# A planner's cost numbers, and with them the order of all instructions, in a linear-attention + MLP kernel on one core

## The chip, the core and the metric

One core of a Trainium2 chip runs the whole program. The metric is the device time of one execution in microseconds (us). Engines: PE (TensorE: matmul, and PEld, its weight loads), DVE (VectorE), ACT (ScalarE), POOL (GpSimd) and SP (SyncE, which issues the transfers). Each engine works through its own queue in order, and waits on semaphores for what others have to finish.

## The reference

```python
def _attn_ref(q, k, v, omega):              # q, k, v: 8 x 8 heads x 576 x 64, omega: 128 x 64
    q_s, k_s = q * scale, k * scale         # scale = 64 ** -0.25
    def phi(x):
        proj = np.einsum('bhsd,md->bhsm', x, omega)
        h = proj - np.sum(x * x, axis=-1, keepdims=True) / 2.0
        h = h - np.max(h, axis=-1, keepdims=True)
        return np.exp(h) / np.sqrt(m)
    q_p, k_p = phi(q_s), phi(k_s)
    kv = np.einsum('bhsm,bhsd->bhmd', k_p, v)
    z = np.sum(k_p, axis=2)
    num = np.einsum('bhsm,bhmd->bhsd', q_p, kv)
    den = np.einsum('bhsm,bhm->bhs', q_p, z)[..., None] + 1e-06
    return num / den

def _moe_ref(x, w_in, w_out):               # x: 4608 x 512 (the attention's output), d_ff 2048
    h = x @ w_in
    g = np.where(h > 0.0, h, np.exp(np.minimum(h, 0.0)) - 1.0)
    return g @ w_out
```

## The kernel before

The 64 heads are worked in 32 pairs. Two batches of four pairs each give a block row of tokens, whose attention output, transposed, is the input x of the MLP. The stages overlap, and by the clock of the profile they are roughly these.

- **Start, 0 to 40 us.** Pairs 0 to 7 are "native": q and k arrive as fp32 on 64 partitions (`load_pair`, L448). For each of a pair's two heads the square of x is written beside it (L483 on ACT, or through the helper of L394 on DVE or POOL), PE projects both with omega (L504, tiles `ppk` and `ppq`, one PSUM bank for each group of four 128-row pieces), DVE takes the row minimum of the negated scores (L512, `nbk`, `nbq`), ACT takes the exponentials (L474, `hk`, `hq`), PE forms K'V (L673, L678, `pkv`) and the sums z (L721, `pz`), DVE the denominators (L740), and PE the numerators (L794, `pn`).
- **Weights, 5 to 160 us.** The MLP weights arrive as 64-bit words and are turned into fp32 (L904 to L935), and split into a rounded high part and a low part.
- **MLP blocks, 120 to 770 us.** Eight blocks of 384 tokens. For each of 16 slices of d_ff: 12 matmuls of 384 columns into `ph` (L983 to L985, high and low parts), the ELU (L992 and L993 on ACT, L996 on DVE), `g` and its low part (L1001, L1004), and 9 matmuls of 512 columns into `acc` (L1017 to L1019).
- **Pairs 8 to 31, beside the MLP blocks.** Here q and k are split into high and low parts too (`tk`, `tq`): the high part is a cast, and the low part, "y_lo", is x minus the high part, 64x576, through the helper of L394, 96 in all (two heads, q and k, 24 pairs). PE projects at L554, DVE takes the row minimum with a product at L568, POOL adds biases (L579, L580), PE forms K'V at L622, z at L718 and the numerators at L842.
- **Last super-blocks, 770 to 1007 us.** The other 1536 tokens go in three blocks of 512 by a Strassen-like scheme, eight steps (j) each. A step computes products into PSUM tiles `A` and `B` (L1369, six matmuls of 256 columns a group; L1339 adds the second layer's part), combines them (`c`, L389 and L1393; L1324 clears the tiles), takes the ELU (L1417, L1422, L1425), splits the seven results `gq` into a high part (cast, ACT) and a low part (helper of L394, POOL or DVE), and multiplies each with its weights into seven sums `acs_1` to `acs_7` (L1527). Their input weights are prepared mostly on DVE from 680 us on (`rw`, `tw`, L394).

**What sets the order.** No instruction order is written out by hand. Every operation is a task that `op()` of the class `Plan` records: an engine and its cost in ns, a due time in us, the tiles it reads and writes, and for some tasks a second engine with its own cost and a handicap (`alt`, table `ALT`). `Plan.order()` walks a simulated clock: on each engine that is free it takes, of the tasks whose inputs are ready, the one with the earliest due time; `mine()` gives a task with two engines to the one that would end it earlier, handicap counted. DVE tasks marked `port` and POOL tasks are not started over each other. Transfers go one after the other through a single channel, with a latency `DMA_LAT` in front, a rate `DMA_RATE` in bytes per ns and a latency behind. Then `issue()` emits all tasks in the order of their simulated starts, and the engines' queues on the chip keep that order whatever the real durations are. So a cost changes nothing in the work: it changes what stands before what on each queue, and, for tasks with an `alt`, the engine.

Of the kernel before, what the change touches and what calls it, by code (L numbers as in the profile page):

```python
# [18 lines left out]
P = 128  # L19
B, H, S, D, M = 8, 8, 576, 64, 128  # L20
# [48 lines left out]
LAG = 3.4  # L69

# [61 lines left out]
class Plan:  # L132
# [14 lines left out]
    DMA_LAT, DMA_RATE = 1100.0, 360.0  # L147
# [33 lines left out]
    def order(self):  # L181
# [7 lines left out]
        end = [0.0] * len(tasks)  # L189
# [3 lines left out]
        slots, dma = {}, 0.0  # L193
# [41 lines left out]
        while len(done) < len(tasks):  # L235
            started = False
            for eng, q in queue.items():
# [37 lines left out]
                if nbytes:  # L275
                    dma = max(now + self.DMA_LAT, dma) + nbytes / self.DMA_RATE
                    end[best] = dma + self.DMA_LAT
                else:
                    end[best] = now + ns
# [34 lines left out]
def mm(n, m=1):  # L314

    return m * (n / 2.4 + 2.5)
# [10 lines left out]
def pool(n):  # L327
    return 40 + 2.33 * n
# [3 lines left out]
def performer_elu_kernel(  # L332
# [52 lines left out]
    op = pl.op  # L385
# [57 lines left out]
    def load_pair(i, due):  # L443
# [7 lines left out]
        for nm, nat, mixed in (("k", k, kx), ("q", q, qx)):  # L451
            if native(i, nm):
                t = s["x" + nm] = Buf(sb, [P, 2, S], F32, "ld" if nm == "k" else "t", f"x{nm}_{i}", 2)
                dma(lambda t=t: t()[0:D], nat[i], P * S * 4, (t, 0), (t, 1))
            else:
                t = s["x" + nm] = Buf(sb, [P, 2, S], F32, "ld", f"x{nm}_{i}", 2)
                dma(lambda t=t: t(), mixed[i - NNAT[nm]], P * S * 8, (t, 0), (t, 3))
# [6 lines left out]
    def project(i, nm, due):  # L464
# [14 lines left out]
        if native(i, nm):  # L479
# [11 lines left out]
            for g in range(3):  # L491
# [17 lines left out]
                op("PE", 872 if g < 2 else 240, d, mms, [*((x, a, 2) for a in range(2)), of], (p,))  # L509
# [21 lines left out]
        for a in range(2):  # L531
# [8 lines left out]
                "POOL", pool(S), due - 4 + a,  # L540
# [3 lines left out]
        for c in range(5):  # L544
# [14 lines left out]
            op("PE", mm(256, n), d, mms, [(y, a, z) for a in range(2) for z in "hl"] + ["oh", "om"], (p,))  # L559
# [14 lines left out]
            if c in (1, 4):  # L574
# [7 lines left out]
                op("POOL", 2 * pool(4), d + 1.3, bias, [sq, *((nb, g, e) for e in range(5))], ((nb, g),))  # L582
# [28 lines left out]
    def kv_swapped(i, due):  # L611
# [15 lines left out]
        op("PE", 5 * 216, due, mms, [*parts, v], (p,))  # L627
# [19 lines left out]
        op("POOL", 3 * pool(2 * M) + 2 * pool(M), due + 0.5, sums, parts, (zs, (zu, 1)))  # L647
# [13 lines left out]
    def kv(i, due):  # L661
# [22 lines left out]
        op("PE", 220, due, last, [*parts, v], ((p, 0), (p, 1)))  # L684
# [17 lines left out]
    def finish(i, due):  # L702
# [25 lines left out]
        for g in range(3):  # L728
# [48 lines left out]
            op("PE", 109 * n, d, turn, ((h, "n", g),), (p,))  # L777
# [19 lines left out]
        op("PE", 4 * mm(S) + 200, d, mms, [*((qh, g) for g in range(3)), ("kvf", i % 2)], [p for _, _, p in halves])  # L797
# [29 lines left out]
    def output(i, qt, due):  # L827
# [8 lines left out]
        def mms():  # L836
# [10 lines left out]
            "PE", 4 * mm(4 * N) + 200, due, mms, [*((qt, g) for g in range(3)), *((zk, "kv", e) for e in range(4))], banks  # L847
# [869 lines left out]
```

## Time and profile before

| what | value |
|---|---|
| time, median of 3 runs (lowest, highest) | 1003.58 us (1001.74, 1006.97) |
| the profiled execution, its own time | 1008.6 us |
| its span in the profile | 1006.8 us |
| PE granted clock, mean | 0.996 of full speed |
| HBM traffic over the span | 223 GB/s |

The profiled execution is one run, 5.0 us above the median; what is read from it is a place or a difference, and the sum has to be brought to the median at the end. A share of busy time is read by stage, as the stages have different limits: for each stage, the length less PE's busy time is what any order could at most win there.

### The profile page before, as it was taken

To read this page: it belongs to the slowest core of one execution; us is meant where nothing else is said; L and a number is where in the kernel's file an instruction comes from. 1 tells how busy PE (TensorE), PEld (TensorE's weight loads), DVE (VectorE), ACT (ScalarE), POOL (GpSimd) and SP (SyncE) were. 2 spreads that over 40 slices of the span, in tenths; PEclk is the share of its full clock that TensorE was granted. 3 is DMA by queue.
4 is the path that set the end of the run, shared out by engine and by line. 5 is a ranking of instruction groups with operands and counts; after the bars stand their busy time and mean duration, and the time that the engine had idled before them with its cause. 6 is when DMAs were issued, how large, how long until landed. Compare 5 with 4: busy or idle time off the path is not lost.

```text
span 1006.8 us, 24315 instructions
## 1 busy us (share of the span) xinstructions
PE 979.3 (97%) x7806; PEld 881.6 (88%) x7806; DVE 843.7 (84%) x3077; ACT 766.2 (76%) x2064; POOL 557.8 (55%) x745
## 2 busy tenths in 40 slices
PE   6999999999999999999999999999999999999997
PEld 5887889888888888888888888887888999999997
DVE  5999978786778967887889888889999889779766
ACT  5999876877568888788887878786555688877774
POOL 0667676776457676677667766685442232223221
PEclk8999999999999999999999999999999999999999
DMA  6656777857766777676776767666888885775762
GB/s 178 181 183 214 238 247 254 270 200 245 232 216 218 232 224 225 202 230 195 252 226 189 242 206 234 203 208 232 268 311 290 289 298 176 238 240 191 239 196 76
DMA packets 93264, 226.27 MB, mean 225 GB/s; under 512 B 23056, under 2 KB 35024, under 8 KB 93136
## 3 DMA queue, kind: packets, MB, share of 16 engines
q1 hardware_dynamic: 93136, 224.70, 69.0%
q8 instruction: 63, 1.03, 0.4%
q14 instruction: 65, 0.53, 0.2%
HBM read 187.43 MB, written 37.22 MB: 223 GB/s over the span
## 4 chain that ended last, share of the span: by engine, by line
PE 69%; DVE 16%; DMA 8%; ACT 3%; issue 2%; SPq 1%; POOL 1%; DVEq 0%; POOLq 0%; ACTq 0%
PE acs L1527 8%; PE ph L983 7%; PE ph L985 6%; PE ph L984 6%; PE acc L1017 6%; PE acc L1018 6%; PE acc L1019 6%; PE A L1369 5%; PE B L1369 4%; PE pn L842 3%; PE pkv L622 2%; PE ppq L554 2%; PE ppk L554 2%; DVE rw L394 2%; DMA rw<-w1s 1%
## 5 line engine op out<-in xcount | busy, mean ns | idle before, releaser
L983 PE MATMUL ph<-xh,w1c 128*128 128x384 f32 x512 | 176.8, 345 | 4.6 <-DVE g L1004 3.0
L984 PE MATMUL ph<-xl,w1c 128*128 128x384 f32 x512 | 172.3, 336 | 1.0 <-DVE xl L807 1.0
L985 PE MATMUL ph<-xh,w1c 128*128 128x384 f32 x512 | 172.3, 336 | 0.0
L1017 PE MATMUL acc<-w2h,g 128*128 128x512 f32 x384 | 154.3, 402 | 0.2
L1018 PE MATMUL acc<-w2l,g 128*128 128x512 f32 x384 | 151.6, 395 | 0.0
L1019 PE MATMUL acc<-w2h,g 128*128 128x512 f32 x384 | 151.5, 394 | 0.0
L983 PEld LDWEIGHTS ph<-xh,w1c 128*128 128x128 f32 x512 | 96.2, 188 | 17.0 <-DVE g L1004 7.3
L984 PEld LDWEIGHTS ph<-xl,w1c 128*128 128x128 f32 x512 | 96.3, 188 | 3.8 <-DVE xl L807 1.4
L992 ACT ACTIVATE e<-ph 128x384 f32<-128x384 f32 x128 | 62.6, 489 | 44.4 <-PE ph L985 43.4
L394 POOL TENSOR_TENSOR hq<-hq,den 128x512 f32<-128x512 f32 (+1 forms) x96 | 81.1, 854 | 27.3 <-DVE den L749 23.5
L985 PEld LDWEIGHTS ph<-xh,w1c 128*128 128x128 f32 x512 | 96.2, 188 | 0.0
L996 DVE SCALAR_TENSOR_TENSOR ph<-e,ph 128x384 f32<-128x384 f32 x128 | 71.2, 556 | 25.5 <-ACT e L993 24.3
L394 POOL TENSOR_TENSOR gq<-yh,gq 128x256 fp32r<-128x256 f32 x49 | 42.7, 871 | 85.1 <-ACT gq L389 67.0
L1019 PEld LDWEIGHTS acc<-w2h,g 128*128 128x128 f32 x384 | 72.1, 188 | 16.9
L1017 PEld LDWEIGHTS acc<-w2h,g 128*128 128x128 f32 x384 | 72.0, 188 | 16.3 <-issue 6.3
L740 DVE CUSTOM_DVE_ANT_0 junk<-hq,pz 128x128 f32<-128x128 f32 (+1 forms) x320 | 74.5, 279 | 11.6 <-PE pz L718 9.3
L394 POOL TENSOR_TENSOR tk<-xk,tk 64x576 fp32r<-64x576 f32 x45 | 64.1, 1424 | 31.5 <-ACT tk L389 12.6
L474 ACT ACTIVATE hk<-hk,nbk 128x128 f32<-128x128 f32 x216 | 68.4, 390 | 17.0 <-POOL nbk L580 16.7
L1018 PEld LDWEIGHTS acc<-w2l,g 128*128 128x128 f32 x384 | 72.1, 188 | 8.6
L474 ACT ACTIVATE hq<-hq,nbq 128x128 f32<-128x128 f32 x216 | 68.5, 391 | 14.4 <-POOL nbq L580 13.6
L394 POOL TENSOR_TENSOR tq<-xq,tq 64x576 fp32r<-64x576 f32 x46 | 65.8, 1431 | 23.6 <-ACT tq L389 11.5
L1004 DVE TENSOR_TENSOR g<-ph,g 128x384 fp32r<-128x384 f32 x128 | 70.4, 550 | 5.7 <-PE pn L842 1.8
(222 smaller groups left out, 2814.7 us busy)
## 6 DMA issues: line engine op xcount, KB each, us to landing
w1c<-w1s SPq DMA_DIRECT2D x112, 512.0 KB, 4.5
wp<-w1t SPq DMA_DIRECT2D x48, 512.0 KB, 4.0
raw_w<-in_w_dram SPq DMA_DIRECT2D x32, 512.0 KB, 4.3
xk<-in_kx_dram SPq DMA_DIRECT2D x24, 576.0 KB, 4.2
xq<-in_qx_dram SPq DMA_DIRECT2D x24, 576.0 KB, 4.7
wp<-w1s SPq DMA_DIRECT2D x24, 512.0 KB, 4.5
v<-in_v_dram SPq DMA_DIRECT2D x32, 325.0 KB, 3.3
w1s<-w1c SPq DMA_DIRECT2D x16, 512.0 KB, 4.2
```

The costliest lines, as they stand in the source:

```text
L394: (nc.vector if e == "DVE" else nc.gpsimd).tensor_tensor(*args)
L474: nc.scalar.activation(h()[:, j, :], src(j), AF.Exp, bias=nb()[:, j:j + 1], scale=-1.0)
L740: nc.vector.tensor_tensor_reduce(out=junk()[r], in0=h()[r, j, :], in1=pz()[r, a * P:(a + 1) * P], scale=1.0, scalar=EPS, op0=ALU.mult, op1 ...
L983: nc.tensor.matmul(ph(), wh, xh[:, c, o:o + n], start=(c == 0), stop=False)
L984: nc.tensor.matmul(ph(), wh, xl[:, c, o:o + n], start=False, stop=False)
L985: nc.tensor.matmul(ph(), wl, xh[:, c, o:o + n], start=False, stop=(c == NC - 1))
L996: lambda: nc.vector.scalar_tensor_tensor(ph(), e()[:, 0:n], -1.0, ph(), ALU.add, ALU.max), (p, e), (p,),
L1017: nc.tensor.matmul(a(), g[0]()[:, ts], w2h[:, f], start=(f == f0), stop=False)
L1018: nc.tensor.matmul(a(), g[0]()[:, ts], w2l[:, f], start=False, stop=False)
L1019: nc.tensor.matmul(a(), g[1]()[:, ts], w2h[:, f], start=False, stop=(f == f1 - 1))
L1369: nc.tensor.matmul(o, at(a, i), u[b][:, i], start=(start and fresh_bank and i == 0 and n == 0), stop=(i == 1 and n == 2), skip_group_check ...
L1527: nc.tensor.matmul(bank()[:, z * TH:(z + 1) * TH], g()[:, a * TH + z * P:a * TH + z * P + P], w(b), start=(j == 0 and z == 0 and m == 0), ...
```

## The change

Only numbers that the planner uses are changed, and one constant is new. A transfer now takes 500 ns in front, 320 bytes per ns, and 2450 ns (`DMA_POST`) behind it, where it had 1100 ns, 360 bytes per ns and 1100 ns; loads of native q and k are planned with twice their bytes. `mm()` gives 113.4 ns for a matmul of 256 columns (109.2 before), 173.1 for 384 (162.5) and 232.9 for 512 (215.8); the tasks of PE that had a number of their own get larger ones. `pool()` and POOL's own numbers change: y_lo is now 1495 ns on POOL (`pool(576)` was 1382). Costs on DVE and ACT stay as they were (y_lo on DVE: 669 ns, and a handicap of 820).

```diff
+DMA_POST = 2450.0
...
-    DMA_LAT, DMA_RATE = 1100.0, 360.0
+    DMA_LAT, DMA_RATE = 500.0, 320.0
...
                     dma = max(now + self.DMA_LAT, dma) + nbytes / self.DMA_RATE
-                    end[best] = dma + self.DMA_LAT
+                    end[best] = dma + DMA_POST
...
 def mm(n, m=1):
-    return m * (n / 2.4 + 2.5)
+    return m * (0.467 * n - 6.2)
...
 def pool(n):
-    return 40 + 2.33 * n
+    return 120 + 2.22 * n
...
-                dma(lambda t=t: t()[0:D], nat[i], P * S * 4, (t, 0), (t, 1))
+                dma(lambda t=t: t()[0:D], nat[i], P * S * 8, (t, 0), (t, 1))
...
-                op("PE", 872 if g < 2 else 240, d, mms, [*((x, a, 2) for a in range(2)), of], (p,))
+                op("PE", 930 if g < 2 else 290, d, mms, [*((x, a, 2) for a in range(2)), of], (p,))
...
-                "POOL", pool(S), due - 4 + a,
+                "POOL", 1495, due - 4 + a,
                 lambda e, r=r, o=o, cs=cs: tt(e, y()[o, cs], x()[r, 0], y()[r, cs].bitcast(F32), ALU.subtract),
                 (*parts, (y, a, "h")), ((y, a, "l"),), alt=other("y_lo", "DVE", dve(S)), port=True,
...
-            op("PE", mm(256, n), d, mms, [(y, a, z) for a in range(2) for z in "hl"] + ["oh", "om"], (p,))
+            op("PE", 118 * n + 10, d, mms, [(y, a, z) for a in range(2) for z in "hl"] + ["oh", "om"], (p,))
...
-                op("POOL", 2 * pool(4), d + 1.3, bias, [sq, *((nb, g, e) for e in range(5))], ((nb, g),))
+                op("POOL", 550, d + 1.3, bias, [sq, *((nb, g, e) for e in range(5))], ((nb, g),))
...
-        op("PE", 5 * 216, due, mms, [*parts, v], (p,))
+        op("PE", 1340, due, mms, [*parts, v], (p,))
...
-        op("POOL", 3 * pool(2 * M) + 2 * pool(M), due + 0.5, sums, parts, (zs, (zu, 1)))
+        op("POOL", 3480, due + 0.5, sums, parts, (zs, (zu, 1)))
...
-        op("PE", 220, due, last, [*parts, v], ((p, 0), (p, 1)))
+        op("PE", 240, due, last, [*parts, v], ((p, 0), (p, 1)))
...
-            op("PE", 109 * n, d, turn, ((h, "n", g),), (p,))
+            op("PE", 115 * n + 20, d, turn, ((h, "n", g),), (p,))
...
-        op("PE", 4 * mm(S) + 200, d, mms, [*((qh, g) for g in range(3)), ("kvf", i % 2)], [p for _, _, p in halves])
+        op("PE", 1250, d, mms, [*((qh, g) for g in range(3)), ("kvf", i % 2)], [p for _, _, p in halves])
...
-            "PE", 4 * mm(4 * N) + 200, due, mms, [*((qt, g) for g in range(3)), *((zk, "kv", e) for e in range(4))], banks
+            "PE", 1400, due, mms, [*((qt, g) for g in range(3)), *((zk, "kv", e) for e in range(4))], banks
```

The added line at the top and one blank line move every later line by two: L474 of before is L476 of the changed kernel, L394 is L396, and so on. Three places in the order follow. A name carries the pair (`xk_1` is K of pair 1), the group (`ppk_1_0` is group 0 of pair 1) and a running number.

**First place: ACT at the start.** Before, the square of pair 1's K stands ahead of the exponentials of pair 0:

```order
L483 ACTIVATE xk_0_162<-xk_0_162 64x576
L398 ACTIVATE of_133<-of_133 64x128
L483 ACTIVATE xq_0_173<-xq_0_173 64x576
L483 ACTIVATE xk_1_177<-xk_1_177 64x576
L474 ACTIVATE hk_0_216<-ppk_0_0_191,nbk_0_205 128x128 x4
L474 ACTIVATE hk_0_216<-ppk_0_1_200,nbk_0_205 128x128 x4
L474 ACTIVATE hk_0_216<-ppk_0_2_211,nbk_0_205 128x128
```

Now the exponentials come first, and ACT no longer squares pair 1's K at all (DVE does both heads):

```order
L485 ACTIVATE xk_0_162<-xk_0_162 64x576
L400 ACTIVATE of_133<-of_133 64x128
L485 ACTIVATE xq_0_173<-xq_0_173 64x576
L476 ACTIVATE hk_0_213<-ppk_0_0_195,nbk_0_207 128x128 x4
L476 ACTIVATE hk_0_213<-ppk_0_1_202,nbk_0_207 128x128 x4
L476 ACTIVATE hk_0_213<-ppk_0_2_209,nbk_0_207 128x128
L485 ACTIVATE xq_1_179<-xq_1_179 64x576
```

**The same place on PE.** Before, the projection of pair 1 (`ppk_1_0`, `ppk_1_1`) stands ahead of K'V of pair 0:

```order
L504 MATMUL ppk_0_0_191<-of_133,xk_0_162 128x128 x4
L504 MATMUL ppk_0_1_200<-of_133,xk_0_162 128x128 x4
L504 MATMUL ppk_0_2_211<-of_133,xk_0_162 64x128 x2
L504 MATMUL ppk_1_0_228<-of_133,xk_1_177 128x128 x4
L504 MATMUL ppk_1_1_235<-of_133,xk_1_177 128x128 x4
L673 MATMUL pkv_0_246<-v_0_175,hk_0_216 128x130
L678 MATMUL pkv_0_246<-v_0_175,hk_0_216 128x65 x8
```

Now half of K'V of pair 0 stands ahead of `ppk_1_0`, and the other half behind it:

```order
L506 MATMUL ppk_0_0_195<-of_133,xk_0_162 128x128 x4
L506 MATMUL ppk_0_1_202<-of_133,xk_0_162 128x128 x4
L506 MATMUL ppk_0_2_209<-of_133,xk_0_162 64x128 x2
L675 MATMUL pkv_0_228<-v_0_175,hk_0_213 128x130
L680 MATMUL pkv_0_228<-v_0_175,hk_0_213 128x65 x4
L506 MATMUL ppk_1_0_236<-of_133,xk_1_177 128x128 x4
L680 MATMUL pkv_0_228<-v_0_175,hk_0_213 128x65 x4
L506 MATMUL ppk_1_1_249<-of_133,xk_1_177 128x128 x4
```

**Second place: the low part y_lo in pairs 8 to 31.** Before, POOL computes both heads of pair 21's K (`x2`):

```order
L394 TENSOR_TENSOR hq_18_6070<-hq_18_6070,den_18_6408 128x128
L394 TENSOR_TENSOR tq_20_6507<-xq_20_6284,tq_20_6507 64x576
L579 TENSOR_TENSOR nbk_20_6576<-nbk_20_6576,sqk_20_6333 128x4
L580 TENSOR_TENSOR nbk_20_6576<-nbk_20_6576,sqk_20_6333 128x4
L394 TENSOR_TENSOR tk_21_6611<-xk_21_6448,tk_21_6611 64x576 x2
L579 TENSOR_TENSOR nbk_20_6576<-nbk_20_6576,sqk_20_6333 128x5
L580 TENSOR_TENSOR nbk_20_6576<-nbk_20_6576,sqk_20_6333 128x5
```

Now POOL has one of the two:

```order
L582 TENSOR_TENSOR nbq_19_6392<-nbq_19_6392,sqq_19_6017 128x5
L396 TENSOR_TENSOR tq_20_6514<-xq_20_6227,tq_20_6514 64x576 x2
L581 TENSOR_TENSOR nbk_20_6560<-nbk_20_6560,sqk_20_6194 128x4
L582 TENSOR_TENSOR nbk_20_6560<-nbk_20_6560,sqk_20_6194 128x4
L396 TENSOR_TENSOR tk_21_6628<-xk_21_6484,tk_21_6628 64x576
L581 TENSOR_TENSOR nbk_20_6560<-nbk_20_6560,sqk_20_6194 128x5
```

and the other stands on DVE, between the row minima of pair 20 and the ELU of slice 70:

```order
L570 ISA nbk_20_6560 128x1
L570 ISA hk_20_6559,nbk_20_6560<-ppk_20_4_6602,p2k_20_4_6621 128x128
L570 ISA nbk_20_6560 128x1
L396 TENSOR_TENSOR tk_21_6628<-xk_21_6484,tk_21_6628 64x576
L998 SCALAR_TENSOR_TENSOR ph_70_6605<-e_70_6643,ph_70_6605 128x384
L393 COPY qt_18_6500<-pn_18_1_6648 128x4x32
L393 COPY qt_18_6500<-pn_18_1_6648 64x32
```

Over all, DVE has 5 of the 96 such instructions before and 31 now.

**Third place: PE, where the super-blocks begin.** Before, the first sum, `acs_1` (of `gq_0_0_1`: super-block 0, step 0, part 1), stands behind the last six matmuls of layer 2 and two groups of step 1 (`wp_0_1_0`):

```order
L1019 MATMUL acc_7_0_0_10798<-w2h_140,g_127_1_11574 128x512
L1369 MATMUL B_11586<-xh_147,wp_0_0_2_11535 128x256 x6
L1369 MATMUL A_11549<-xh_147,wp_0_1_0_11601 128x256 x6
L1017 MATMUL acc_7_0_1_10808<-w2h_140,g_127_0_11566 128x512
L1018 MATMUL acc_7_0_1_10808<-w2l_141,g_127_0_11566 128x512
L1019 MATMUL acc_7_0_1_10808<-w2h_140,g_127_1_11574 128x512
L1017 MATMUL acc_7_0_2_10817<-w2h_140,g_127_0_11566 128x512
L1018 MATMUL acc_7_0_2_10817<-w2l_141,g_127_0_11566 128x512
L1019 MATMUL acc_7_0_2_10817<-w2h_140,g_127_1_11574 128x512
L1369 MATMUL B_11586<-xh_147,wp_0_1_0_11601 128x256 x6
L1527 MATMUL acs_1_11714<-w2h_140,gq_0_0_1_11676 128x256
```

Now it stands ahead of all of them:

```order
L1529 MATMUL acs_1_11671<-w2l_141,gq_0_0_1_11634 128x256
L1529 MATMUL acs_1_11671<-w2h_140,gq_0_0_1_11634 128x256 x2
L1529 MATMUL acs_1_11671<-w2l_141,gq_0_0_1_11634 128x256
L1529 MATMUL acs_1_11671<-w2h_140,gq_0_0_1_11634 128x256
L1019 MATMUL acc_7_0_1_10813<-w2h_140,g_127_0_11574 128x512
L1020 MATMUL acc_7_0_1_10813<-w2l_141,g_127_0_11574 128x512
L1021 MATMUL acc_7_0_1_10813<-w2h_140,g_127_1_11584 128x512
L1019 MATMUL acc_7_0_2_10863<-w2h_140,g_127_0_11574 128x512
L1020 MATMUL acc_7_0_2_10863<-w2l_141,g_127_0_11574 128x512
L1021 MATMUL acc_7_0_2_10863<-w2h_140,g_127_1_11584 128x512
L1371 MATMUL A_11550<-xh_147,wp_0_1_0_11611 128x256 x6
L1371 MATMUL B_11595<-xh_147,wp_0_1_0_11611 128x256 x6
```

The rest of that order reads as above with groups of `acs` one or two places earlier against the groups of `A` and `B`.

## Rows read from the trace of the kernel before

**Rows 1.** the page's part 1: busy us, share of the span, instructions
```profile
PE 979.3 (97%) x7806; PEld 881.6 (88%) x7806; DVE 843.7 (84%) x3077; ACT 766.2 (76%) x2064; POOL 557.8 (55%) x745
```

**Rows 2.** the page's part 4: the chain that ended last, share by engine
```profile
PE 69%; DVE 16%; DMA 8%; ACT 3%; issue 2%; SPq 1%; POOL 1%; DVEq 0%; POOLq 0%; ACTq 0%
```

**Rows 3.** busy time by stage: window, length, engines' us (instructions), PE clock, DMA share, GB/s
```profile
0.00:40.00 40.00, 30.63 (x220) 27.64 (x221) 27.35 (x91) 27.11 (x77) 11.02 (x16) 0.91 0.63 177
40.00:160.00 120.00, 116.52 (x746) 98.56 (x745) 108.40 (x330) 101.69 (x253) 82.40 (x75) 1.00 0.69 221
160.00:680.00 520.00, 515.71 (x4226) 452.45 (x4225) 425.51 (x1935) 414.80 (x1124) 359.64 (x524) 1.00 0.70 223
680.00:770.00 90.00, 86.99 (x629) 75.69 (x630) 87.05 (x230) 47.52 (x126) 38.37 (x53) 1.00 0.78 272
770.00:820.00 50.00, 48.29 (x402) 46.75 (x401) 44.54 (x117) 38.46 (x110) 16.13 (x18) 1.00 0.88 303
820.00:1007.00 187.00, 181.14 (x1590) 180.51 (x1588) 150.85 (x379) 136.62 (x378) 50.24 (x62) 1.00 0.62 197
```

**Rows 4.** PE's waits, whole span: engine, line, waited for; us, times, longest
```profile
PE ppk L504 <- ACT hk L474: 5.4, 1, 5.4
PE ph L983 <- DVE g L1004: 3.0, 7, 0.7
```

**Rows 5.** timeline of PE, 3 to 20 us: start, us, instruction [idle before]
```profile
5.65 2.42 PE L504 MATMUL ppk<-of,xk 128*128 128x128 f32 x20 [0.94 <-ACT of L398]
13.52 3.78 PE L504 MATMUL ppk<-of,xk 128*128 128x128 f32 x16 [5.44 <-ACT hk L474]
17.09 0.64 PE L673 MATMUL pkv<-v,hk 128*128 128x130 f32 x2
17.52 2.62 PE L678 MATMUL pkv<-v,hk 128*128 128x65 f32 x16
```

**Rows 6.** timeline of ACT, 3 to 20 us
```profile
11.61 0.68 ACT L483 ACTIVATE xk<-xk 64x576 f32<-64x576 f32 x1 [2.80 <-DMA xk<-in_k_dram]
12.32 2.44 ACT L474 ACTIVATE hk<-ppk,nbk 128x128 f32<-128x128 f32 x9
```

**Rows 7.** timeline of DVE, 3 to 20 us
```profile
8.91 0.69 DVE L512 TENSOR_REDUCE nbk<-ppk 128x4 f32<-128x512 f32 x1
11.62 0.75 DVE L394 TENSOR_TENSOR xk<-xk 64x576 f32<-64x576 f32 x1 [2.01 <-DMA xk<-in_k_dram]
12.40 0.89 DVE L512 TENSOR_REDUCE nbk<-ppk 128x4 f32<-128x512 f32 x2
13.32 1.42 DVE L394 TENSOR_TENSOR xq<-xq 64x576 f32<-64x576 f32 x2
```

**Rows 8.** groups of tile tk, 150 to 650 us: ns min/median/max, starts, form
```profile
L394 POOL TENSOR_TENSOR tk<-xk,tk x39: 1408/1422/1442, 192.3 to 637.4; 64x576 fp32r<-64x576 f32 x39
L394 DVE TENSOR_TENSOR tk<-xk,tk x3: 756/1279/1750, 194.7 to 615.5; 64x576 fp32r<-64x576 f32 x3
```

**Rows 9.** busy time of two windows by themselves, columns as in rows 3
```profile
520.00:560.00 40.00, 40.00 (x357) 35.07 (x356) 35.02 (x189) 32.55 (x90) 29.23 (x46) 1.00 0.71 226
...
720.00:770.00 50.00, 48.62 (x312) 42.89 (x312) 48.07 (x99) 25.32 (x62) 14.69 (x17) 1.00 0.81 291
```

**Rows 10.** timeline of PE, 770 to 775 us
```profile
771.27 0.87 PE L1369 MATMUL A<-xh,wp 128*128 128x256 f32 x6
771.97 0.39 PE L1017 MATMUL acc<-w2h,g 128*128 128x512 f32 x1
...
773.37 0.85 PE L1369 MATMUL B<-xh,wp 128*128 128x256 f32 x6
774.05 0.28 PE L1527 MATMUL acs<-w2h,gq 128*128 128x256 f32 x1
```

**Rows 11.** timeline of POOL, 765 to 773 us
```profile
772.12 0.93 POOL L394 TENSOR_TENSOR gq<-yh,gq 128x256 fp32r<-128x256 f32 x1 [8.68 <-ACT gq L389]
```

**Rows 12.** DMA issues of 0 to 25 us: KB each, median us to landing
```profile
xk<-in_k_dram SPq DMA_DIRECT2D x4, 288.0 KB, 5.5
```

## The prediction

> **What bounds the kernel now.** I read the shares of the engines first, then the chain that ended last, then the busy time by stage, then PE's waits, and at the end the timelines of the places that the new order touches. PE is busy for 979.3 of 1006.8 us [rows 1], and the chain that ended last runs through PE for 69% and through DVE for 16% [rows 2]. The reader should see from this that an order, which adds no work and takes none away, can win at most the time in which PE stands still: 1006.8 less 979.3, so 27.5 us. By stage, each window's length less PE's busy time [rows 3], that is 9.4 us in 0 to 40, 3.5 in 40 to 160, 4.3 in 160 to 680, 3.0 in 680 to 770, 1.7 in 770 to 820 and 5.9 after that. The clock is at full speed from 40 us on (1.00), so nothing is to be had there. Of PE's waits only one is long: 5.4 us, once, on the first exponentials of ACT. The next, on `g` from DVE, is 3.0 us in seven pieces of at most 0.7 [rows 4]. In 520 to 560 PE is busy for 40.00 of 40 us [rows 9]: in the middle of the kernel there is nothing to gain, only something to lose. So the change is looked at in three places: the start, the middle with its cover, and the super-blocks.
>
> **The costs themselves.** New numbers for PE cost nothing on the chip; the matmuls take what they took. What they do is to let the simulated PE arrive later than before against ACT and DVE, whose numbers stay. The planner then thinks that work of ACT and DVE is ready sooner, by PE's count, and puts what reads it earlier into PE's queue. For a transfer of native K (294,912 bytes) the plan goes from 1100 + 819 + 1100 = 3.0 us to 500 + 1843 + 2450 = 4.8 us; the trace has 5.5 us as the median of the four in the first 25 us [rows 12]. So that part of the plan comes nearer to the trace. The first 14 transfers on SP's queue stand as before, and later ones change places with a neighbour; I cost that at nothing, since the two longest lines of PE's waits name no transfer [rows 4]; if a load came late, it would be seen as a wait of a `ph` or `ppk` matmul.
>
> **The start: 1.4 us gained.** Before, ACT waits 2.80 us for pair 1's K, squares it at 11.61, and only then, at 12.32, begins the nine exponentials of pair 0 (2.44 us for all) [rows 6]. DVE does the same thing: its second row minimum of pair 0 stands behind the square at 11.62 [rows 7]. PE waits 5.44 us for this, to 13.52 [rows 5]. In the new order the first row minimum, 8.91 + 0.69 = 9.60, releases the exponentials, since ACT no longer has the square ahead of them: they run from 9.60 and end at about 9.60 + 2.44 = 12.0. PE's first projection ends at 5.65 + 2.42 = 8.07 [rows 5], so PE stands still from 8.07 to about 12.0, 4.0 us and not 5.44. Then it does half of K'V of pair 0, 1.6 us of the 3.1 that its eighteen matmuls take (17.09 to 17.52 + 2.62) [rows 5]. `ppk_1_0` is not held up behind it: the load is there at 11.62, and two squares on DVE take about 1.42, as the two of q do [rows 7], so it is ready at 13.0, before PE comes to it. Gain: 5.44 - 4.0 = 1.4 us. The bounds are 0, if the weights' conversion or ACT's queue, which follow at once, take up what was won, and 2.7 us (12.32 - 9.60), if everything behind the exponentials moves with them. I take 1.4, because it is the part that PE itself shows.
>
> **The middle: nothing, with a bound of +4.7.** Of 96 y_lo instructions 5 stand on DVE before and 31 now, 26 more. On POOL one takes 1.42 us; on DVE 0.76, 1.28 and 1.75 (three records) [rows 8]. DVE gets 26 x 0.76 = 20 us at the least, 26 x 1.28 = 33 us by the median, 26 x 1.75 = 45.5 us at the most, on 425.5 of 520 [rows 3]: 86%, 88% or 91%. The nearest row for the middle value is the window 520 to 560, where DVE is at 35.02 of 40, 88%, and PE still stands at 40.00; in 720 to 770 DVE is at 96% and PE stands still for 1.38 of 50, 2.8% [rows 9]. So at 88% I take 0. Between the two rows, 91% is a third of the way, so 0.9% of the stage's 520 us, +4.7, for the upper bound. What hides the 33 us is DVE's own idle time, which is work that PE does not need yet; if it is gone, the `g` that the matmuls of layer 1 and 2 wait for is late next, and all that stands behind a y_lo on DVE with it. POOL gives off 26 x 1.42 = 37 us, of which nothing shows on the time, as the two longest lines of PE's waits name ACT and DVE [rows 4].
>
> The same rows say something on how the two engines share a port: the DVE form varies between 0.76 and 1.75 us for one shape, and the longest is about as much over the shortest (1.0) as a good part of one POOL instruction (1.42) [rows 8]. The Trainium skill, page "SBUF — State Buffer", section "Who interferes with whom", says that a DVE instruction with two SBUF inputs and a GpSimd instruction that reads SBUF lock each other out for the whole instruction, and whichever comes second waits. By that rule the moved instructions would cost near the upper end, since POOL is still busy for most of the time, and the middle would cost about +4.7 instead of 0; the trace agrees as to the spread (0.76 to 1.75). It speaks against this change.
>
> **The super-blocks: 1.8 us lost.** In the trace `acs_1` begins at 774.05; the `A` group that now stands behind it began at 771.27 [rows 10]. Between them lie that group, six matmuls of layer 2 and one `B` group: 774.05 - 771.27 = 2.78 us of cover that goes. The low part it reads was finished by POOL at 772.12 + 0.93 = 773.05 [rows 11], 1.0 us before its use. So PE would wait 2.78 - 1.0 = 1.8 us here, and what was moved behind it does not fill that. In the same way other groups of `acs` lose cover: in steps 1 and 7 of the first super-block and steps 0 and 7 of the second, four more places. I take these four at nothing, as each loses one or two groups of six (0.68 us each, by 774.05 - 773.37 [rows 10]) and a wait once paid gives later ones their cover back; the bounds are 0 for all five, and 1.8 for each, 8.9 us.
>
> **The sum.** -1.4 + 0 + 1.8 = +0.4 on the profiled execution's own 1008.6, so 1009.0. That execution stands 5.0 above the median of 1003.58, so the forecast for the median is 1004.0.
>
> **The rivals.** *First, the new order fits the chip better (faster).* The start brings its bound, 2.7; the other waits of 40 to 680, 3.5 + 4.3 = 7.8, are halved (3.9), since inputs are no longer planned for sooner than they land; and half of 680 to 820's 4.7 goes (2.4). That makes -9.0, so 994.6. For it: the plan of transfers and of PE comes nearer to the trace. Against it: after the first wait, the next line is made of pieces of 0.7 us at most [rows 4], so there is little in one place to win. *Second, the super-blocks run short (slower).* All five places pay 1.8, and the start gives 1.4: +7.5, so 1011.1. It decides where DVE and ACT take as long from the products to `gq` as in the trace of before, so that no place has cover to spare. For it: DVE is busy for 44.54 of 50 us in 770 to 820 [rows 3], and the plan makes DVE and ACT look quicker than they are, more so now against PE. Against it: the waits are one after the other, and the first one covers the next. *Third, DVE becomes the bound in the middle (slower).* The lock takes the upper value at each of the 26, +4.7 with the rest as forecast: 1008.7, and more if they fall together; it decides from about 90% of DVE on. *Fourth, nothing happens:* PE is saturated and gains and losses are taken up within 1 us, 1003.6.
>
> **How the numbers follow.** The forecast has 0.38; the first rival 0.22, the second 0.18, the third 0.16, the fourth 0.06. About 0.5%, 5 us, is what a measurement of this kernel can tell from no change, so below 998.6 is faster and above 1008.6 slower. Faster comes from the first rival alone, 0.22. The forecast and the fourth give 0.44 for no change. The second and the third, whose 1008.7 lies just past the bound, give 0.34. The range goes from 995, the first rival's end, to 1013, the second rival's 1011.1 and part of what the second and the third make together (1004.0 + 4.7 + 7.1 = 1015.8). The cases of no change alone have 1000 to 1008.
>
> **What would show it.** In the profile of the changed kernel the exponentials of pair 0 should begin near 9.6 us and not 12.3, and the long wait of PE should be 4.0. DVE's busy time should be 20 to 45 us up, POOL's 37 down, and PE's wait on `g` (3.0 us) should not be over 4. A wait of 1 to 2 us before the first `acs_1` near 772 should be new. I am wrong if PE stands still for more than 8 us in 160 to 680, if the waits of `acs` come to over 4 us, or if the sum of PE's idle time (27.5) changes by more than 5.

## The result, and the profile after

The changed kernel takes 1016.71 us (median of 4 runs, 1014.22 to 1019.06) against 1004.62 for the kernel before in the same runs (1001.74 to 1006.97): a ratio of 1.0121, with a 95% interval of 1.008 to 1.0162. It is slower by 12 us, where 1004.0 in a range of 995 to 1013 had been forecast. The profiled execution took 1019.06 us, its span is 1017.3, 10.5 more than that of before.

The page's part 1 of the changed kernel answers to [rows 1]:

```profile
PE 988.0 (97%) x7806; PEld 886.7 (87%) x7806; DVE 871.5 (86%) x3137; ACT 757.7 (74%) x2035; POOL 523.5 (51%) x714
```

The same 7806 matmuls keep PE busy for 8.7 us longer, and its idle time grows by 1.8 only (1017.3 - 988.0 = 29.3, before 27.5). So PE's idle time, on which the prediction was built, shows a sixth of the loss: the rest lies inside what the records call busy. A stage's length less PE's busy time, then, is not all that an order can win or lose there. By stage, with the columns of [rows 3]:

```profile
0.00:40.00 40.00, 34.62 (x229) 30.43 (x230) 26.92 (x93) 28.88 (x82) 12.36 (x17) 1.00 0.68 197
40.00:160.00 120.00, 113.09 (x714) 95.56 (x713) 104.76 (x312) 93.52 (x233) 75.37 (x64) 0.97 0.62 206
160.00:680.00 520.00, 513.97 (x4217) 450.42 (x4217) 456.21 (x1992) 408.47 (x1089) 327.47 (x497) 1.00 0.69 222
```

DVE is at 456.21 of 520 us in the middle (before 425.51), POOL at 327.47 (359.64). Between 40 and 160 the clock is no longer at 1.00 but at 0.97. PE's waits, against [rows 4]:

```profile
PE ph L985 <- DVE g L1006: 5.1, 8, 1.5
PE pt L766 <- DVE nbk L570: 3.5, 2, 3.0
...
PE pn L796 <- DVE den L742: 1.5, 1, 1.5
```

The long wait of the start is gone, and a wait of 3.0 us in one piece, of `pt` for `nbk`, is new. The timeline of PE shows its place (start, us, instruction, idle before):

```profile
118.25 0.34 PE L986 MATMUL ph<-xl,w1c 128*128 128x384 f32 x1
118.42 0.34 PE L987 MATMUL ph<-xh,w1c 128*128 128x384 f32 x1
...
120.98 0.60 PE L766 MATMUL pt<-ident,hq 128*128 128x128 f32 x4
124.55 0.45 PE L766 MATMUL pt<-ident,hq 128*128 128x128 f32 x1 [2.98 <-DVE nbk L570]
124.93 0.69 PE L985 MATMUL ph<-xh,w1c 128*128 128x384 f32 x1
125.42 0.52 PE L986 MATMUL ph<-xl,w1c 128*128 128x384 f32 x1
125.73 0.52 PE L987 MATMUL ph<-xh,w1c 128*128 128x384 f32 x1
```

And these windows show what follows, the granted clock being the column behind POOL's:

```profile
120.00:124.00 4.00, 1.57 (x9) 1.06 (x8) 3.90 (x8) 0.64 (x2) 1.78 (x2) 0.95 0.35 112
123.50:124.00 0.50, 0.00 (x0) 0.00 (x0) 0.50 (x3) 0.50 (x2) 0.00 (x0) 0.61 0.65 129
124.00:128.00 4.00, 3.45 (x11) 2.50 (x13) 3.05 (x13) 3.45 (x9) 1.47 (x3) 0.50 0.97 360
128.00:132.00 4.00, 4.00 (x17) 2.70 (x14) 1.67 (x3) 1.92 (x5) 2.48 (x3) 0.70 0.37 135
```

PE stands still for 2.98 us, and then runs at 0.50, that is at 1.2 GHz and not 2.4: matmuls of 384 columns follow each other every 0.31 us (125.42 to 125.73), and not every 0.17 (118.25 to 118.42). By the clock column that is (0.05 x 4 + 0.50 x 4 + 0.30 x 4) / 0.5 = 6.8 us at half speed. The clock is down from 123.6, while PE still stands, so 0.9 us of them belong to the wait; the other 5.9 us cost 2.9 us besides the 2.98 (an estimate). DVE's timeline says why it was late:

```profile
116.77 1.81 DVE L929 SCALAR_TENSOR_TENSOR u_w<-raw_w,u_w 128x512 int32<-128x512 int32 x1
118.61 1.48 DVE L396 TENSOR_TENSOR tq<-xq,tq 64x576 fp32r<-64x576 f32 x1
120.12 0.51 DVE L917 TENSOR_SCALAR u_w<-u_w 128x512 f32<-128x512 f32 x1
120.66 1.74 DVE L396 TENSOR_TENSOR tq<-xq,tq 64x576 fp32r<-64x576 f32 x1
...
123.24 0.75 DVE L393 COPY p2k<-ppk 128x256 f32<-128x256 f32 x2
123.91 0.28 DVE L570 CUSTOM_DVE_ANT_0 hk<-ppk,p2k 128x128 f32<-128x128 f32 x1
```

Two y_lo of pair 8's q, one of 1.48 us and one of 1.74, and a step of the weights' conversion that takes 1.81 stand ahead of the row minima of pair 8 (L570), after which a bank of PSUM that `ppk` and `pt` share is free for `pt`. In the kernel before only one y_lo of pair 8 stands there, and PE's wait is 1.03 us, on another tile, with the granted clock at 1.00 from 120 to 128 us:

```profile
121.89 1.73 DVE L394 TENSOR_TENSOR tq<-xq,tq 64x576 fp32r<-64x576 f32 x1
126.29 0.45 PE L984 MATMUL ph<-xl,w1c 128*128 128x384 f32 x1 [1.03 <-DVE xl L807]
```

The groups of `tk` in the changed kernel, against [rows 8]:

```profile
L396 POOL TENSOR_TENSOR tk<-xk,tk x19: 1414/1427/2117, 184.3 to 664.4; 64x576 fp32r<-64x576 f32 x19
...
L396 DVE TENSOR_TENSOR tk<-xk,tk x29: 751/755/1725, 103.8 to 663.2; 64x576 fp32r<-64x576 f32 x29
```

With 6 of `tq`, DVE has 35 y_lo and not 31 as counted ahead of the prediction (four rows of the order hold two each), so 30 were moved and not 26; and most take 0.755 us there.

### The profile page after: what moved, and what is told of

Its sections match the earlier page's. It is cut to its first block, busy times and chain, and to the rows that moved or that the text cites. A ratio compares the mean times of both kernels' runs of the same rounds, so it can differ in the third digit from the quotient of the medians.

```text
span 1017.3 us, 24288 instructions
## 1 busy us (share of the span) xinstructions
PE 988.0 (97%) x7806; PEld 886.7 (87%) x7806; DVE 871.5 (86%) x3137; ACT 757.7 (74%) x2035; POOL 523.5 (51%) x714
## 3 DMA queue, kind: packets, MB, share of 16 engines
q8 instruction: 63, 1.03, 0.4%
## 5 line engine op out<-in xcount | busy, mean ns | idle before, releaser
L985 PEld LDWEIGHTS ph<-xh,w1c 128*128 128x128 f32 x512 | 96.5, 189 | 20.7 <-DVE g L1006 10.3
L396 POOL TENSOR_TENSOR hq<-hq,den 128x512 f32<-128x512 f32 (+1 forms) x96 | 81.4, 857 | 23.1 <-DVE den L751 21.4
L998 DVE SCALAR_TENSOR_TENSOR ph<-e,ph 128x384 f32<-128x384 f32 x128 | 71.1, 556 | 21.5 <-ACT e L995 20.7
L396 POOL TENSOR_TENSOR gq<-yh,gq 128x256 fp32r<-128x256 f32 x50 | 42.1, 841 | 81.0 <-ACT gq L391 74.7
L1019 PEld LDWEIGHTS acc<-w2h,g 128*128 128x128 f32 x384 | 72.2, 188 | 12.6 <-issue 3.5
L932 POOL TENSOR_TENSOR u_w<-u_w,raw_w 128x512 int32<-128x512 int32 x32 | 44.2, 1384 | 67.1 <-DVE u_w L929 32.3
L476 ACT ACTIVATE hq<-hq,nbq 128x128 f32<-128x128 f32 x216 | 68.4, 391 | 12.8 <-POOL nbq L582 12.5
L396 POOL TENSOR_TENSOR gq<-y,gq 128x256 fp32r<-128x256 f32 x30 | 25.4, 846 | 92.6 <-ACT gq L391 86.2
L476 ACT ACTIVATE hk<-hk,nbk 128x128 f32<-128x128 f32 x216 | 68.3, 391 | 5.5 <-POOL nbk L582 5.1
```

Of the source, the lines that this page charges most:

```text
L396: (nc.vector if e == "DVE" else nc.gpsimd).tensor_tensor(*args)
L476: nc.scalar.activation(h()[:, j, :], src(j), AF.Exp, bias=nb()[:, j:j + 1], scale=-1.0)
L985: nc.tensor.matmul(ph(), wh, xh[:, c, o:o + n], start=(c == 0), stop=False)
L998: lambda: nc.vector.scalar_tensor_tensor(ph(), e()[:, 0:n], -1.0, ph(), ALU.add, ALU.max), (p, e), (p,),
L1019: nc.tensor.matmul(a(), g[0]()[:, ts], w2h[:, f], start=(f == f0), stop=False)
```

## The experiments

Each ratio is to the kernel before on the same chip, with its 95% interval.

**e1 to e3: each part of the change by itself.** The edits are those of the diff: in e1 the three on transfers, in e2 `mm()` and PE's seven numbers, in e3 `pool()` and POOL's three.

> The kernel before with only the transfer numbers changed (500, 320, 2450 and the doubled bytes of native loads). 6 of the 96 low parts y_lo stand on DVE, as good as before (5). Theory (the 12 us come from y_lo on DVE among the weights' conversion near 120 us, where PE stops about 3 us for DVE and then runs some us at half its clock): no such stop, ratio to before 0.997 to 1.005. Rival A (PE's durations put PE's reads too early): same, ratio about 1.00. Rival B (the later landings reorder loads and conversions, and that makes the stop near 120 us): the stop is here, ratio 1.006 or more.

> The kernel before with only PE's numbers changed (mm and the seven numbers of its own tasks). 6 of 96 y_lo on DVE. Theory (y_lo on DVE): no stop of 3 us near 120, ratio 0.997 to 1.005. Rival A (PE's durations): the loss is here, ratio 1.008 to 1.015, with waits of acs, A and B in the super-blocks adding to over 4 us. Rival B: ratio about 1.00.

> The kernel before with only POOL's numbers changed (pool(), y_lo 1495, biases 550, sums 3480). 23 of 96 y_lo on DVE. Theory (y_lo on DVE): ratio 1.005 to 1.012, with a stop of PE for DVE of over 1.5 us between 100 and 135 us. Rivals A and B: ratio about 1.00, no stop.

Measured: e1 1.0287 (1.0263 to 1.031), e2 1.0339 (1.0304 to 1.0373), e3 1.0127 (1.0106 to 1.0148). Each part alone is as bad as the whole or far worse, and e1 and e2 lose 29 and 35 us with 6 y_lo on DVE. So y_lo is not the cause by itself, and the parts do not add up. Rival A said about 1.00 for e1, rival B about 1.00 for e2: neither part holds the loss alone. Nor does a stop need the moved y_lo: e1, with 6 on DVE, stands near 120 us as well, and its granted clock is down to 0.50 from 120 to 128.

```profile
116.00:120.00 4.00, 2.35 (x11) 1.43 (x13) 3.97 (x20) 2.51 (x6) 0.00 (x0) 0.73 0.90 314
120.00:124.00 4.00, 3.43 (x14) 2.07 (x11) 3.65 (x13) 2.68 (x6) 3.19 (x3) 0.50 0.72 262
124.00:128.00 4.00, 4.00 (x14) 4.00 (x14) 4.00 (x16) 2.36 (x6) 3.92 (x6) 0.50 0.94 330
```

**e4: the change with y_lo kept on POOL.**

```diff
-ALT = dict(..., y_lo=0.82, ...)
+ALT = dict(..., y_lo=2.5, ...)
```

> The whole change, and y_lo's handicap on DVE 2.5 for 0.82, which leaves 6 of 96 there for 35. Theory (y_lo on DVE): the stop near 120 us and the slow clock behind it go, 6 us or more of the 12 come back, ratio 1.000 to 1.006. Rivals A and B: the loss stays, ratio 1.009 to 1.015.

Measured: 1.0107 (1.0087 to 1.0126). The stop is gone, as these windows of e4 show (PE busy for all of them, clock 1.00), and still only 1.4 us came back, less than the intervals can tell apart:

```profile
120.00:124.00 4.00, 4.00 (x23) 3.75 (x22) 2.64 (x4) 2.25 (x6) 3.81 (x3) 1.00 0.77 275
124.00:128.00 4.00, 4.00 (x24) 3.72 (x23) 3.32 (x7) 2.78 (x5) 2.19 (x2) 1.00 0.99 370
```

The planner's other choices moved with the handicap, and what the stop had cost was lost elsewhere; where, no run shows. So the theory of the stop falls as the whole explanation. The ratio is the one that rivals A and B had named for e4, but e1 and e2 had spoken against both.

**e5 and e6: which numbers belong together.** e5 is the change without POOL's numbers; e6 the whole change, with `act()` and `dve()` times 1.1.

> The whole change without POOL's numbers; 6 of 96 y_lo on DVE. The runs so far: transfers alone 1.029, PE's durations alone 1.034, POOL's numbers alone 1.013, the whole 1.012. Theory M (what counts is how the engines' costs stand to each other and to the transfers: PE's and the transfers' numbers belong together): ratio 1.005 to 1.018, near the whole change. Theory F (due times and handicaps are fitted to the old numbers, and every other set of numbers gives some order that they do not fit, with a loss that has nothing to do with the size or truth of the edit): anywhere from 1.008 to 1.035, and the two small edits of this call lose as well.

> The whole change, and DVE's and ACT's costs times 1.1 as well, so that all engines' numbers have grown together. Theory M: most of the loss comes back, ratio 0.998 to 1.006. Theory F: it stays lost, ratio 1.008 or more, since the due times fit this set no better.

Measured: e5 1.0334 (1.0311 to 1.0357), e6 1.0083 (1.0059 to 1.0107). Transfers and PE together are as bad as each alone; all engines' numbers together are a little better than the change, but nearly all of the loss stays.

**e7 and e8: edits that mean nothing.**

```diff
-    return m * (n / 2.4 + 2.5)
+    return m * (n / 2.4 + 2.5) * 1.005
```

```diff
-    DMA_LAT, DMA_RATE = 1100.0, 360.0
+    DMA_LAT, DMA_RATE = 1100.0, 358.0
```

> The kernel before with mm() times 1.005: a matmul of 384 columns is planned with 163.3 ns for 162.5, an edit that means nothing. Theory M and the theory of y_lo on DVE: ratio 0.998 to 1.003. Theory F: a loss like those of the parts, ratio 1.006 to 1.03.

> The kernel before with a transfer rate of 358 for 360, the other edit that means nothing. Theory M and the theory of y_lo on DVE: ratio 0.998 to 1.003. Theory F: ratio 1.006 to 1.03.

Measured: e7 1.0256 (1.0224 to 1.0288), e8 1.0166 (1.0132 to 1.0199). An edit of half a per cent on one cost loses 26 us, more than twice what the change loses. PE's waits in e7:

```profile
PE ph L983 <- DVE g L1004: 8.9, 5, 2.5
PE acc L1017 <- ACT o L389: 5.0, 3, 3.5
PE pkv L622 <- DVE nbq L568: 2.1, 1, 2.1
```

No place stands out; the waits are of the kinds that the other kernels have, more and longer. Theory M falls, and theory F is what the four runs agree with: the due times and the handicaps fit the old numbers so closely that half a per cent undoes it. That it is the fit, and not that any other order is worse, is tested by e14 to e18.

**e9 to e12: one stretch of the order at a time.** No planning anew here. The order of before is kept, and the tasks of one stretch stand in the order, and on the engines, of the changed kernel (here e10):

```diff
+FIRST, LAST = 220, 1190
...
-        for n, eng in self.order():
+        order = self.order()
+        order[FIRST:LAST] = [(int(w[1:]), ENG[w[0]]) for w in STRETCH.split()]
+        for n, eng in order:
```

> The kernel before, with the first 220 tasks (to about 36 us) in the order and on the engines of the changed kernel, all later ones as before. Theory C (the 12 us are made in 110 to 135 us, where DVE's four y_lo of pair 8 stand among the weights' conversion, and PE stops and loses its clock): -1 to -3 us. Theory S (the loss is spread over all stretches in small pieces): -1 to -3 us too; both traces show PE some 1.5 us ahead at 40 us.

> The kernel before, with tasks 220 to 1190 (about 36 to 214 us) as in the changed kernel. Theory C: +6 to +10 us, most of the loss, with the stop of PE near 125 us and a granted clock of 0.5 behind it. Theory S: +2 to +4.

> The kernel before, with tasks 1190 to 4150 (about 214 to 664 us) as in the changed kernel, 21 more y_lo on DVE among them. Theory C: 0 to +3 us. Theory S: +3 to +5. If y_lo on DVE is what hurts in the middle, PE's wait on g grows here.

> The kernel before, with tasks from 4150 on (about 664 us to the end, with the super-blocks) as in the changed kernel. Theory C: 0 to +2 us. Theory S: +3 to +5, with a wait of acs_1 of 1 to 2 us near 772 us.

Measured: e9 1.0023 (1.0007 to 1.004), e10 1.0093 (1.0074 to 1.0111), e11 1.0046 (1.0027 to 1.0064), e12 1.0085 (1.0064 to 1.0106). In us that is +2.3, +9.3, +4.6 and +8.5. The stop comes back in e10, within 0.02 us of its length:

```profile
121.70 0.60 PE L823 MATMUL pt<-ident,hq 128*128 128x128 f32 x4
125.26 0.30 PE L823 MATMUL pt<-ident,hq 128*128 128x128 f32 x1 [2.96 <-DVE nbk L627]
```

So that place is real, and it is the dearest; but e12 is nearly as dear, and the four sum to some 25, twice the 12.1 of the whole. Theory C is right in e10 and too low in e11 and e12, theory S is right in e11 and too low in e10 and e12, and both had a gain for e9. (By its trace e11 has 25 more y_lo on DVE, not 21.) A seam between two orders is an order that no plan made, so each of the four may be too high; that is argued, not shown. A count without seams: take for each PE task its usual step (median of start to next start for its line, in the trace of before), and call lost what the trace takes beyond the sum of the steps. One execution each, us lost:

| stretch, us | order of before (trace of before, then those of e9 to e12 that keep it) | order of the change (its trace, then the one of e9 to e12) | difference of means |
|---|---|---|---|
| 0 to 40 | 9.9, 8.1, 6.9, 7.4 | 8.4, 7.0 | -0.4 |
| 40 to 200 | 2.2, 2.5, 2.0, 2.4 | 8.6, 8.7 | +6.4 |
| 200 to 680 | 8.5, 9.4, 10.9, 10.7 | 11.3, 11.1 | +1.3 |
| 680 to 1000 | 11.1, 8.4, 10.8, 9.9 | 12.6, 13.6 | +3.0 |

That sums to +10.3, where the two spans differ by 10.5. Over half of this loss is made between 40 and 200 us, and in the changed kernel's trace the 2.98 + 2.9 us at 125 are most of that. In e10's the clock column is 0.73 and 0.84 for 124 to 132 us, which costs 1.7 us and not 2.9, so there more of the 8.7 lies elsewhere in the stretch.

**e13: the one move that the prediction priced.** The order of before, and 30 y_lo on DVE.

```diff
-            self.tasks[n][2](eng)
+            self.tasks[n][2]("DVE" if n in TO_DVE else eng)
```

> The order of the kernel before, task for task; only the 30 y_lo that the change moves go to DVE instead of POOL, each at its old place in the order. Nothing else moves. By the prediction's term: 0 to +4.7 us, ratio 1.000 to 1.005. If y_lo on DVE is the main cause of the 12 us: 1.008 or more. PE's wait on g should grow from 3 us.

Measured: 1.0071 (1.0047 to 1.0095), so +7.1 us (4.7 to 9.5): above the prediction's bound, and short of 1.008. PE's wait on `g` grew, from 3.0 us in seven pieces to 5.3 in twelve. That wait, and the middle window with the columns of [rows 3]:

```profile
PE ph L985 <- DVE g L1006: 5.3, 12, 0.8
...
160.00:680.00 520.00, 514.58 (x4209) 449.29 (x4208) 444.01 (x1957) 412.71 (x1120) 325.65 (x496) 1.00 0.69 222
```

DVE went from 425.51 to 444.01, and PE stands still for 5.42 and not 4.29. The other 6 us are not to be found in PE's idle time of this window.

**e14 to e16: the tables searched anew.** Some 75 numbers, the due times and the handicaps, were varied at random and kept where the planner, under the costs given, finished sooner; no run on the chip took part. e14 has the change's costs, e15 those of e7, e16 those of e6. Of e14, two lines of many:

```diff
-SEG = [6.25, 7.76, 3.48, 4.4, 2.75, 6.34]
+SEG = [6.092, 7.761, 3.496, 4.357, 2.608, 8.103]
...
-DUE_LOAD, DUE_K, DUE_KV, DUE_Q = 9.63, 24.93, 17.79, 16.94
+DUE_LOAD, DUE_K, DUE_KV, DUE_Q = 7.666, 19.134, 16.693, 16.393
```

> The changed kernel with all its costs as they are, and the due times and handicaps searched anew for them (the criterion is the planner's own finish under these costs, no run on the chip). Theory F (the loss is that the old tables do not fit the new numbers): the 12 us come back, ratio to before 0.985 to 1.003. If the new numbers themselves make worse orders (they are less true, or DVE's and ACT's that stayed are too low against them): ratio 1.006 or more.

> The edit that means nothing (mm() times 1.005, ratio 1.026 with the old tables), with the tables searched anew in the same way. Theory F: the loss goes, ratio 0.995 to 1.006. If 1.026 has to do with the matmul cost itself: it stays above 1.015.

> The whole change with DVE's and ACT's costs times 1.1 too (1.008 with the old tables), and the tables searched anew. Theory F: as the changed kernel refitted or better, as all engines' numbers are nearer to the trace: ratio 0.980 to 1.000. If truth of the numbers counts for nothing beside the fit: the same as the other refitted kernels within 0.5%.

Measured: e14 0.9982 (0.9967 to 0.9997), e15 1.0032 (1.0007 to 1.0056), e16 1.0043 (1.0024 to 1.0063). All three come back to within half a per cent of the kernel before, from 1.012, 1.026 and 1.008. The same window of e14:

```profile
160.00:680.00 520.00, 515.32 (x4301) 451.60 (x4300) 461.39 (x2114) 403.09 (x1057) 348.63 (x530) 1.00 0.69 220
```

DVE is busier here than in the changed kernel (461.39 against 456.21). A full DVE is no loss by itself; what counts, it seems, is whether what stands ahead in its queue is wanted first. e15 is also the nearest thing to a search under the old costs, which was not run: it ends at 1.003, so there searching anew won nothing by itself. One expectation failed: e16 lies outside the 0.980 to 1.000 that theory F had for it, and nearer to the other reading, that truer numbers count for nothing beside the fit.

**e17 and e18: the pairing, and luck.** e17 has the costs of before and e14's tables; e18 the change's costs and tables from a second search.

> The fourth corner: the costs of the kernel before with the due times and handicaps of e14, which were searched for the changed kernel's costs. Theory F (numbers and tables belong together): a loss as for any pair that was not searched together, ratio to before 1.006 to 1.03. If e14's tables are simply better: ratio 1.00 or less.

> The changed kernel's costs with tables from a second search that began elsewhere at random. Theory F: near e14, ratio 0.990 to 1.006. If e14's 0.998 was luck of one order out of many: anywhere up to 1.02.

Measured: e17 1.0184 (1.0165 to 1.0203), e18 1.005 (1.0032 to 1.0068). e14's tables are not better by themselves: under the old numbers they lose as the old tables lose under the new. The four corners are 1.000 (old, old), 1.012 (new numbers, old tables), 1.018 (old numbers, new tables) and 0.998 (new, new). And y_lo on DVE are not what was wrong with the changed kernel's order: e18 has 55 of the 96 there, 20 more than the change, and loses less than half as much.

```profile
L396 DVE TENSOR_TENSOR tk<-xk,tk x37: 751/754/1765, 95.2 to 651.9; 64x576 fp32r<-64x576 f32 x37
L396 DVE TENSOR_TENSOR tq<-xq,tq x18: 753/754/1853, 113.1 to 624.9; 64x576 fp32r<-64x576 f32 x18
```

The misfit can be read without the chip. `Plan.order()`, worked through by itself with the numbers that stand in each kernel, ends its simulated clock at 916.6 us for the kernel before and 928.0 for e17; at 938.0 for e7 and 914.8 for e15; at 989.5 for the change, 973.8 for e14 and 976.4 for e18; at 1007.8 for e6 and 991.4 for e16. In each of these four groups, which share their costs, the earlier finish is the faster kernel by the medians; finishes under different costs say nothing of each other. (e4, at 990.5, cannot be told from the change.) For e7 the planner itself ends 21.5 us later than for the kernel before, where half a per cent on every cost would be 4.6.

e14 is the one version that was measured below both kernels, by 0.2% against the kernel before. The second search under the same costs gave 1.005, so which tables a search ends on is worth more than that gain. That the truer numbers are worth anything once fitted is not shown: e16, with DVE and ACT nearer to the trace as well (y_lo on DVE 736 ns for 669, measured 755), is behind e14.

## Why the prediction was wrong

**"New numbers for PE cost nothing", and the loads "at nothing".** This step failed first. That a cost alters no instruction's work is true, and so the loss was looked for only at the places where a move could be read in the order. But the planner re-decides everything: alone, PE's numbers cost 35 us (e2) and the transfers' 29 (e1), and e7 moves nothing on purpose and loses 26. What should have stood there is a term for the fit that is given up, and the rival "any other set of numbers loses" was missing from the list. All eight of e1 to e8 lost, by 0.8% to 3.4%.

**The start, -1.4.** The order does what was said: the exponentials run at 8.43 (forecast 9.6), and PE's wait is 1.59 us:

```profile
8.43 1.14 ACT L476 ACTIVATE hk<-ppk,nbk 128x128 f32<-128x128 f32 x4 [1.16 <-DVE nbk L514]
11.58 0.80 PE L675 MATMUL pkv<-v,hk 128*128 128x130 f32 x2 [1.59 <-ACT hk L476]
```

The gain is not there: e9 gives +2.3 us, the count above -0.4. The term was sized on one execution's late load. In e10 to e13 the start is the order of before, task for task; of e11 and e12:

```profile
9.40 0.68 ACT L674 ACTIVATE xk<-xk 64x576 f32<-64x576 f32 x1 [1.87 <-DMA xk<-in_k_dram]
10.10 2.43 ACT L665 ACTIVATE hk<-ppk,nbk 128x128 f32<-128x128 f32 x9
```

```profile
10.42 0.68 ACT L626 ACTIVATE xk<-xk 64x576 f32<-64x576 f32 x1 [2.46 <-DMA xk<-in_k_dram]
11.13 2.43 ACT L617 ACTIVATE hk<-ppk,nbk 128x128 f32<-128x128 f32 x9
```

The K of pair 1 was squared at 11.61 in the trace of before [rows 6], at 9.40 and 10.42 here, 9.80 in e13 and 11.05 in e10; PE waited 5.44 us there [rows 5], and 1.7, 4.3, 1.8 and 3.0 in these four. That the profiled execution was 4 us above the median of this comparison partly for this reason is likely, not shown. If so, taking 1.4 us off and then bringing the sum to the median, 5.0 lower, took the same late load off twice.

**The middle, 0 with a bound of +4.7.** y_lo on DVE was a move worth pricing, and the price was too low: with the order around it kept, it costs 7.1 us (e13). The step that failed is "at 88% I take 0". It read from PE's 40.00 of 40 in one window [rows 9] that nothing is lost there; but PE's busy time is no measure of work done, as part 1 of the changed kernel shows: 8.7 us more for the same matmuls. The Trainium skill, page "Perfetto Trace Analysis", section "Identifying the Most-Contended Engine", warns that the busy share of matmuls is not a good measure of how close a kernel is to its roofline, because pipelined instructions look smaller in the trace. The trace agrees with the warning and not with the direction: the same 7806 matmuls look longer here, by the 8.7 us. The term was also taken over 160 to 680, though part of the moved instructions stand before that, where DVE is nearly full: in 40 to 160 it has 108.40 of 120 us [rows 3]. The stop at 125 us was not on the list for this reason. One sign set ahead did fail: PE's wait on `g` was to stay at or under 4 us, and came to 5.1. The third rival, DVE as the bound with 1008.7, had named such waits; but e14 and e18 have a fuller DVE and no such loss.

The Trainium skill's rule on the shared port ("SBUF — State Buffer", "Who interferes with whom") agrees with the trace where the two engines meet: at the stop, with POOL at work from 117.97 to 121.78 us, y_lo on DVE take 1.48 and 1.74 us, and there the rule's price was nearer than 0. Over all, 29 records of `tk` have a median of 0.755, so most of them paid nothing for the lock. That fits a planner which does not start the two over each other, and the price by the rule left this out.

**The super-blocks, +1.8.** The move is there, the wait is not. In the changed kernel `acs_1` follows its `B` group without a gap:

```profile
777.28 0.87 PE L1371 MATMUL B<-xh,wp 128*128 128x256 f32 x6
777.99 0.28 PE L1529 MATMUL acs<-w2h,gq 128*128 128x256 f32 x1
...
780.09 0.87 PE L1371 MATMUL A<-xh,wp 128*128 128x256 f32 x6
781.69 0.97 PE L1371 MATMUL B<-xh,wp 128*128 128x256 f32 x6 [0.73 <-ACT B L1328]
```

Its low part was ready, ended by POOL at 775.91; the step set the old landing (773.05) against the new place in the queue, though all that makes the low part moved too. The longest wait of PE near it is 0.73, on the clearing of `B`, now on ACT. The stretch from 664 us on loses 8.5 us by e12, or 3.0 by the count; not at the places named, and no single wait holds it. Where inside it the time goes is left open.

**The sum and the rivals.** +0.4 was forecast, 12.1 came. The second rival, with 1011.1, is nearest in number but not in cause: it had five waits of `acs` of 1.8 us each, and all of them come to 0.8. None of the three tests set ahead would have called the prediction wrong: PE stands still for 6.0 us in 160 to 680 (8 allowed), its waits of `acs` stay at 0.8 (4 allowed), and its idle time goes from 27.5 to 29.3 (5 allowed). All three read PE's idle time, which shows a sixth of the loss.

## What to carry to other kernels

Where a scheduler with fitted tables makes the order, costs and tables are one thing: after any edit of a cost, even towards the truth, search the tables anew before the edit is judged, compare the scheduler's own finish under the same costs, and judge an edit against one that means nothing (here 0.5% on a matmul: 1.026) as well as against no edit. Size a wait from several executions where a load ends it, and bring the sum to the median only for what that execution did not already show. Judge PE by how far its steps run over their usual length, not by how long it is busy.

## What the runs showed of the hardware

A wait of PE can cost more than its length: in a standstill of 2.98 us the granted clock fell to 0.50, it was 0.50 for 124 to 128 us, and the half speed cost 2.9 us more. The kernel before has the same at its start, where PE stood for 5.44 us:

```profile
12.00:14.00 2.00, 0.48 (x2) 0.48 (x3) 1.94 (x5) 1.98 (x8) 0.00 (x0) 0.55 1.03 404
14.00:18.00 4.00, 4.00 (x21) 4.00 (x21) 2.45 (x7) 2.56 (x8) 0.00 (x0) 0.50 0.46 140
18.00:24.00 6.00, 4.97 (x39) 4.45 (x38) 4.48 (x10) 4.97 (x16) 1.29 (x1) 0.91 0.23 61
```

In the changed kernel the clock stays at 1.00 there, after a wait of 1.59. The length of the wait alone does not settle it: e11 and e13 have the same order at the start and waits of 1.72 and 1.77, and this granted clock, e11 first:

```profile
12.00:14.00 2.00, 2.00 (x13) 1.94 (x12) 1.48 (x4) 1.51 (x6) 0.00 (x0) 0.63 1.04 416
```

```profile
12.00:14.00 2.00, 2.00 (x19) 1.94 (x18) 1.96 (x6) 1.53 (x6) 0.00 (x0) 1.00 1.03 412
```

Over a whole run the clock explains little of the change's 12 us (mean 0.995 and 0.996 in the two profiled executions), but more of others. The mean granted clock of e1's four executions is 0.987, of e17's five 0.987, and of the kernel before beside them 0.997 and 0.996: at half speed for the difference, that is some 10 us of e1's 29 and 9 of e17's 19 (an estimate, and an upper one, as the clock is also down while PE waits).

And the square that waits for the first load of a second K began at 9.40, 9.80, 10.42, 11.05 and 11.61 us in five executions with the same order up to there.
